# Attention with chosen key chunks and a gated FFN on one core: the first pairs' k and q loaded three tokens side by side and turned head by head, the guard value as a step of its own, and a new order of the steps

## The chip, the cores and the metric

The kernel runs on one core of a Trainium2 chip. The core has five engines with instruction streams of their own: TensorE (PE in the profile, with PEld for its weight loads), VectorE (DVE), ScalarE (ACT), GpSimd (POOL) and SyncE (SP). SP, ACT and POOL also issue DMA transfers, which run on 16 DMA engines. The metric is device time of one execution in microseconds (us). Three runs of the kernel before took 319.53, 315.69 and 314.50 us, median 315.69.

## The reference

There are 4 batches of 8 heads, 768 tokens and head size 64. Keys are cut into 24 chunks of 32. For every query an upper bound of its score with each chunk is worked out from the smallest and largest key of the chunk; the six chunks with the highest bounds are kept, and attention runs over those alone, causally. The result, 3072 tokens by 512, goes through a normalisation and a gated FFN of width 1536.

```python
k_min, k_max = np.min(k_chunks, axis=3), np.max(k_chunks, axis=3)
ub = np.sum(np.maximum(q * k_min, q * k_max), axis=-1)      # per query and chunk
ub = np.where(causal, ub, -1e9)
top_chunks = np.argsort(ub, axis=-1)[..., -6:]
scores = scale * (q @ k.T);  mask = sel & (pos[:, None] >= pos[None, :])
attn = softmax(np.where(mask, scores, -1e9));  x = attn @ v
xn = x / sqrt(mean(x * x) + 1e-6) * rms_g
out = (silu(xn @ w_gate) * (xn @ w_val)) @ w_out
```

## The kernel before, in words

The work is cut into 16 pairs of heads, four pairs to a batch, and the FFN into eight halves of a batch (384 tokens each). Every piece of work is a "step" with a name, an engine or a choice of engines, the steps it depends on and the buffers that it opens and uses. The order of the steps, the engine of each and the slot of each new buffer stand in one long text, PROGRAM (lines 28 to 149): "P153:6" is step 153 on TensorE with its buffer in slot 6, and A, D, G and S are ACT, DVE, POOL and SP. `Order.run` follows the text word by word. Each engine runs its own steps in that order. So an engine never overtakes in its own queue, and a step that waits holds up everything behind it on the same engine.

For each pair, `prep` does the following.

- **Load** (L497): k and q of both heads come in as [128 partitions, 6 tiles, 2 heads, 64 values] in fp32. Partition p of tile t holds token 128 t + p, so one contiguous piece is the 64 values of a token, 256 bytes. Pair 0 is loaded in two halves, one head from SP's queue and the other from ACT's; the other pairs have one DMA a head from SP. The buffers of kind "nat" have 7 slots.
- **Turn** (L517): three tiles go into one PSUM bank by three fp32 transposes of 128 by 128 (both heads at once), which gives the head's values on the partitions and tokens along the row. There are two such banks in a tensor. They are evicted to SBUF (helper `evict`, L289 on ACT and L293 on DVE or POOL) as "kt" and "qt".
- **Bounds**: smallest and largest key of each chunk (L546, L548, DVE), their difference (`dif`, L599), the positive part of q ("relu", L633 on ACT or L635 on DVE), then small fp32 matmuls "ub" (L723; L781 for two pairs at once from pair 6 on). The ub matmuls use parts of the array: 64 rows (a head) by 32 columns, six or eight of them side by side. The bounds are copied out, turned back ("up", L747 or L803), and the causal mask is added (L762, L810).
- **Choice**: MAX8 finds the eight highest bounds (L650). The step "sel" then does two things on DVE: it compares each bound with the sixth highest (L665 or L674), and it writes one more column, the guard value max(highest - 480, 0) (L668 or L679).
- **Placing the choice**: for pairs 0 to 2 TensorE turns the choice ("selT", L694) and DVE copies it beside the query values ("selC"). From pair 3 on, q is laid out by a cast ("qN"), the choice is written beside it, and a DMA transpose (L557) turns both together; that buffer, "qn", has two slots. The keys carry matching constant rows (`e_all`; SP copies them at L385 and L386 into the sets of buffers that pairs use).

`scores` then makes score groups of up to 512 columns (L868, with the triangular mask of batch 0 added by a matmul at L874), exponentials on ACT (L885) and the products with v (L904). The v loads are DMAs that POOL issues (L473), and so are the six weight loads (L437 for gate and value, L442 for out). `norm` and `ffn` work batch by batch: gate steps L1037, value steps L1058, out steps L1078.

Fillers (L338) are matmuls on a tile of zeros. There are 88 such steps to choose from, and PROGRAM may leave them out; this one uses 34. All other work of TensorE is needed.

Of the kernel before, what the change touches and what calls it, by code (L numbers as in the profile page):

```python
# [198 lines left out]
def kernel(  # L199
# [25 lines left out]
    W = S // 2  # L225
    G = 3
    DUO = 6
    KSIDE, QM = 16, 3
    HW = NT * P + D
    NPAIRS = B * NP  # L230

# [51 lines left out]
    def pe(n):  # L283
        return 0.003 + n / 2400.0
# [56 lines left out]
    for i in range(BUSY):  # L341
        bank = Buf("ps")
        add("busy", "PE", pe(4 * P), 1000.0 + i, busy(bank, 4 * P), [c_zero], opens=[bank])
# [806 lines left out]
```

## Time and profile before

| | |
|---|---|
| runs shown | 314.50, 315.69, 319.53 us |
| the profiled execution | 314.75 us, of which the instructions span 313.0 |
| TensorE busy | 303.2 us, 97% |
| DVE, ACT, POOL busy | 231.5, 185.5, 103.9 us |
| granted TensorE clock | 0.997 of full |
| read from HBM, written | 28.57 MB, 6.29 MB |

A group line of the page gives the source line, engine and operation, what is written and read with its shape, then how often, the busy time in us, the mean in ns, and the idle time of the engine before it with what ended it. A timeline line gives start and length in us, and in brackets idle time with its releaser. In the table by stretches the columns are TensorE, its weight loads, DVE, ACT and POOL with counts, then the granted clock, the mean number of busy DMA queues for an engine, and GB/s. Lengths of matmuls overlap: the next one starts before the one before has ended, so their number and the chain say more than the sum of lengths.

### The profile page before, as it was taken

To read this page: it belongs to the slowest core of one execution; us is meant where nothing else is said; L and a number is where in the kernel's file an instruction comes from. 1 tells how busy PE (TensorE), PEld (TensorE's weight loads), DVE (VectorE), ACT (ScalarE), POOL (GpSimd) and SP (SyncE) were. 2 spreads that over 40 slices of the span, in tenths; PEclk is the share of its full clock that TensorE was granted. 3 is DMA by queue.
4 is the path that set the end of the run, shared out by engine and by line. 5 is a ranking of instruction groups with operands and counts; after the bars stand their busy time and mean duration, and the time that the engine had idled before them with its cause. 6 is when DMAs were issued, how large, how long until landed. Compare 5 with 4: busy or idle time off the path is not lost.

```text
span 313.0 us, 7431 instructions
## 1 busy us (share of the span) xinstructions
PE 303.2 (97%) x2772; PEld 191.7 (61%) x2790; DVE 231.5 (74%) x654; ACT 185.5 (59%) x415; POOL 103.9 (33%) x162
## 2 busy tenths in 40 slices
PE   7998999999999999999999999999999999999994
PEld 3676776576576855667687546656666545555541
DVE  4998989969985789856978879989544564577551
ACT  1688998783298773697794643366697403442001
POOL 8686453371354843252377100033233110000000
PEclk9999999999999999999999999999999999999998
DMA  9999999999699996797684060361240034100014
GB/s 173 220 190 126 96 191 206 201 165 168 129 185 198 220 114 146 175 191 138 138 68 28 17 140 13 52 77 36 58 79 36 2 78 155 69 3 0 2 67 169
DMA packets 113301, 35.35 MB, mean 113 GB/s; under 512 B 106225, under 2 KB 110065, under 8 KB 113265
## 3 DMA queue, kind: packets, MB, share of 16 engines
q1 hardware_dynamic: 83152, 26.62, 41.1%
q0 software_dynamic: 28512, 7.87, 24.9%
q10 hardware_dynamic: 1600, 0.39, 0.6%
q8 instruction: 22, 0.36, 0.5%
q14 instruction: 15, 0.11, 0.1%
HBM read 28.57 MB, written 6.29 MB: 111 GB/s over the span
## 4 chain that ended last, share of the span: by engine, by line
PE 87%; DMA 5%; DVE 4%; POOL 1%; issue 1%; SPq 1%; ACT 1%; POOLq 0%
PE po L1078 20%; PE vp L1058 19%; PE gp L1037 19%; PE sc L868 9%; PE av L904 5%; DMA wv<-in_moe_w_val_dram 4%; PE pk L517 3%; PE busy L338 3%; PE pq L517 3%; PE ub L781 2%; PE ub L723 2%; PE up L803 1%; DMA qs<-qn 1%; DVE m L650 1%; DVE qs L293 1%
## 5 line engine op out<-in xcount | busy, mean ns | idle before, releaser
L885 ACT ACTIVATE pt<-sc 128x512 bf16<-128x512 f32 (+2 forms) x192 | 92.9, 561 | 17.5 <-PE sc L868 15.4
L1044 ACT ACTIVATE sg<-gp 128x384 bf16<-128x384 f32 x96 | 45.5, 496 | 55.1 <-PE gp L1037 42.2
L1050 DVE SCALAR_TENSOR_TENSOR tg<-sg,gp 128x384 bf16<-128x384 bf16 x96 | 51.8, 550 | 32.0 <-ACT sg L1044 30.6
L1058 PE MATMUL vp<-xT,wv 128*128 128x384 bf16 x384 | 74.0, 326 | 0.3 <-DMA wv<-in_moe_w_val_dram 0.2
L1037 PE MATMUL gp<-xT,wg 128*128 128x384 bf16 x384 | 73.2, 326 | 0.7 <-ACT xT L289 0.4
L1078 PE MATMUL po<-wo,hh 128*128 128x512 bf16 x272 | 66.9, 379 | 0.9 <-issue 0.2
L1066 DVE TENSOR_TENSOR hh<-vp,tg 128x384 bf16<-128x384 f32 x96 | 51.6, 552 | 12.6 <-PE vp L1058 11.7
L868 PE MATMUL sc<-qs,ke 128*128 128x128 bf16 (+5 forms) x420 | 57.1, 251 | 0.3 <-DMA qs<-qn 0.2
L1058 PEld LDWEIGHTS <-wv 128*128 128x128 bf16 x384 | 35.9, 98 | 25.0 <-issue 1.2
L1037 PEld LDWEIGHTS <-wg 128*128 128x128 bf16 x384 | 36.2, 98 | 23.9 <-issue 1.5
L1078 PEld LDWEIGHTS <-hh 128*128 128x128 bf16 x288 | 27.3, 98 | 29.1 <-issue 1.5
L904 PEld LDWEIGHTS <-pt 128*128 128x128 bf16 x672 | 35.1, 98 | 10.5 <-ACT pt L885 0.6
L904 PE MATMUL av<-vx,pt 128*128 128x65 bf16 x672 | 41.4, 193 | 0.1
L891 POOL TENSOR_SCALAR_AFFINE_SELECT pt<-pt 128x512 bf16<-128x512 bf16 (+1 forms) x48 | 24.4, 521 | 47.4 <-ACT pt L885 43.6
L868 PEld LDWEIGHTS <-ke 128*128 128x128 bf16 (+1 forms) x420 | 30.6, 97 | 9.6 <-issue 1.6
L293 POOL CAST ke<-kt 64x768 bf16<-64x768 f32 x32 | 26.6, 835 | 16.6 <-ACT kt L289 6.0
L293 POOL CAST qn<-qnat 128x768 bf16<-128x768 f32 x13 | 10.7, 822 | 40.5 <-DMA qs<-qn 40.5
L291 ACT ACTIVATE osb<-po 128x512 f32<-128x512 f32 x12 | 7.1, 599 | 24.7 <-PE po L1078 24.7
L981 DVE SCALAR_TENSOR_TENSOR xs<-xb,ri,gains 128x512 bf16<-128x512 bf16 x24 | 17.5, 751 | 2.1 <-POOL ri L973 1.7
L925 DVE TENSOR_TENSOR xb<-av,rden 128x384 bf16<-128x384 f32 (+1 forms) x34 | 18.2, 534 | 1.2
L473 POOL DMA_DIRECT2D vx<-in_v_dram x16 | 16.9, 1055 | 0.1
L650 DVE MAX8 m<-ubm 128x8 f32<-128x8 f32 (+4 forms) x192 | 16.7, 160 | 0.2
(83 smaller groups left out, 297.7 us busy)
## 6 DMA issues: line engine op xcount, KB each, us to landing
out_dram<-osb SPq DMA_DIRECT2D x24, 256.0 KB, 2.3
knat<-in_k_dram SPq DMA_DIRECT2D x30, 192.0 KB, 4.3
qnat<-in_q_dram SPq DMA_DIRECT2D x30, 192.0 KB, 4.6
vx<-in_v_dram POOLq DMA_DIRECT2D x16, 192.0 KB, 5.5
wg<-in_moe_w_gate_dram POOLq DMA_DIRECT2D x2, 768.0 KB, 11.6
wv<-in_moe_w_val_dram POOLq DMA_DIRECT2D x2, 768.0 KB, 10.0
wo<-in_moe_w_out_dram POOLq DMA_DIRECT2D x2, 768.0 KB, 10.1
qs<-qn SPq DMA_TRANSPOSE x26, 2.8
```

The costliest lines, as they stand in the source:

```text
L293: engine[e].tensor_copy(out_, in_)
L650: nc.vector.max(out=m8.tile[:, y[0], y[1], :], in_=ubm.tile[:, y[0], y[1], 0:max(8, 4 * (i0 + x) + 4)])
L868: nc.tensor.matmul(t[:, x:x + m, :].rearrange("p a b -> p (a b)"), ke[kk, kb * P:(kb + 1) * P], qs[kk, q0 * P:(q0 + m) * P], start=not tri ...
L885: nc.scalar.activation(out=t[:, 0:nn, :], in_=sc.tile[:, 0:nn, :], func=ACT.Exp, scale=SCALE)
L891: nc.gpsimd.affine_select(out=pt.tile[:, 0:nd, :], in_=pt.tile[:, 0:nd, :], compare_op=ALU.is_ge, fill=0.0, base=0, pattern=[[0, nd], [1, ...
L904: nc.tensor.matmul(av.tile[:, qi - i0, :], pt.tile[:, x, :], VX[c.v.slot][:, hl * NT + kb, :], start=(begin and m == 0), stop=(left[0] == ...
L1037: nc.tensor.matmul(t[:], wg[:, g, hs], XT[b].tile[:, g, cols], start=(g == 0), stop=(g == NP - 1))
L1044: nc.scalar.activation(out=t[:], in_=gp.tile[:], func=ACT.Tanh, scale=0.5)
L1050: nc.vector.scalar_tensor_tensor(out=t[:], in0=sg.tile[:], scalar=1.0, in1=gp.tile[:], op0=ALU.add, op1=ALU.mult)
L1058: nc.tensor.matmul(t[:], wv[:, g, hs], XT[b].tile[:, g, cols], start=(g == 0), stop=(g == NP - 1))
L1066: nc.vector.tensor_tensor(out=t[:], in0=vp.tile[:], in1=tg.tile[:], op=ALU.mult)
L1078: nc.tensor.matmul(po.tile[:], hhs[ht].tile[:, th * P:(th + 1) * P], wo[:, ht, :], start=(ht == 0), stop=(ht == NHT - 1))
```

## The change

There are four parts.

1. k of pairs 0 to 3 and q of pairs 0 to 2 are loaded so that partition p of a group of 384 tokens holds the tokens 3p, 3p+1 and 3p+2 one after the other: one contiguous piece has 768 bytes.
2. Those tensors are turned by plain fp32 matmuls against the identity in place of transposes: for each of three columns of tokens and each head, 64 stationary columns on 128 moving ones, head 0 into the columns 0 to 63 of the array and head 1 into 64 to 127. That is six matmuls a bank in place of three. The eviction puts the columns back in the order of tokens, writing every third column.
3. The guard value leaves "sel" and becomes a step "grd", which ACT, POOL or DVE may do. ACT needs a constant column `cap` of -480 for it.
4. POOL may do "relu", and PROGRAM is a new one.

Also new is a way to load v through SP and a cast; its list of pairs, VDIRECT, is empty, so it isn't used.

The new order uses 6 fillers, all at the beginning. Its first loads are q and k of pair 0 by halves in turn, q and k of pair 1, k of pair 2, q of 3, k of 6, k of 3; the constant key rows come behind these, where before they stood behind the loads of pair 1 and k of 3. TensorE turns k of pair 0, one bank of q of pair 1, q of pair 0, k of pair 1 and a bank of k of pair 2 ahead of the first "ub"; by the first score it has turned ten banks of k and seven of q, where the order before has eight and four. Of the guards 5 are on ACT, 9 on POOL and 2 on DVE; 5 relus are on POOL, 8 on ACT (12 before) and 3 on DVE (4 before). POOL issues both gate loads, then a q cast, then the first value load; before it was gate, value, gate, behind that cast. The FFN begins with 7 gate steps instead of 4.

```diff
+    K3, Q3 = 4, 3
+    VDIRECT = ()
...
+    cap = const.tile([P, 1], FP32, name="cap")
+    c_cap = add("cap", "DVE", 0.07, -98, lambda e: nc.vector.memset(cap[:], -GUARD))
...
+            three = p < (K3 if w == "k" else Q3)
...
+                if three:
+                    if nat[w].tile is None:
+                        tile_of(nat[w], [P, NT // 3, 2, 3 * D], FP32, w + "nat")
+                    for hl in range(2):
+                        eng = nc.scalar if p == 0 and hl else nc.sync
+                        eng.dma_start(out=nat[w].tile[:, r0 // 3:(r0 + rn) // 3, hl, :],
+                                      in_=src[b, h0 + hl, r0 * P:(r0 + rn) * P].rearrange(
+                                          "(g p s) d -> p g (s d)", p=P, s=3))
+                    return
...
+                    if three:
+                        for j in range(3):
+                            for h in range(2):
+                                nc.tensor.matmul(
+                                    t[h * D:(h + 1) * D, j * P:(j + 1) * P],
+                                    nat[w].tile[:, j0 // 3, h, j * D:(j + 1) * D], ident_f[:],
+                                    start=True, stop=True, tile_position=(0, h * D))
+                        return
...
+                    if three:
+                        evict(e, big[w].tile[:, j0 * P:(j0 + 3) * P].rearrange("p (x s) -> p s x", s=3),
+                              bank.tile[:].rearrange("p (s x) -> p s x", s=3))
+                        return
...
-                nc.vector.tensor_scalar(
-                    out=s12[:, :, NCH:NCH + 1], in0=m12[:, :, 0:1], scalar1=-GUARD,
-                    scalar2=0.0, op0=ALU.add, op1=ALU.max)
...
+            def guard(e):
...
+                o, m = s12[:, :, NCH:NCH + 1], m12[:, :, 0:1]
+                if e == "ACT":
+                    nc.scalar.activation(out=o, in_=m, func=ACT.Relu, bias=cap[:, 0:1])
+                else:
+                    engine[e].tensor_scalar(out=o, in0=m, scalar1=-GUARD, scalar2=0.0,
+                                            op0=ALU.add, op1=ALU.max)
...
-            sT = add("selT", "PE", nb * 0.057, rank(at, b, "selT"), sel_turn, [pk, c_idb], opens=[st], uses=[sq])
+            sT = add("selT", "PE", nb * 0.057, rank(at, b, "selT"), sel_turn, [pk, gd, c_idb], opens=[st], uses=[sq])
```

More of the change, by code (lines that the diff above doesn't have):

```diff
@@ L470, in load_v, with get @@
         b, h0 = c.b, c.h0
+        if c.p in VDIRECT:
+            vn = Buf("nat")
+            def get(e):
+                t = tile_of(vn, [P, 2 * NT, D], FP32, "vnat")
+                nc.sync.dma_start(out=t[:], in_=v[b, h0:h0 + 2].rearrange("h (t p) d -> p (h t) d", p=P))
+            x = add("vget", "SP", 1.0, rank(lr, b, "vload"), get, opens=[vn], load=S * 550)
+            c.vload = add("vC", "", {"POOL": pool(2 * NT * D), "DVE": 0.5, "ACT": act(2 * NT * D)},
+                          rank(lr, b, "vload"), lambda e: evict(e, VX[c.v.slot][:, :, 0:D], vn.tile[:]),
+                          [x] + c_vx, opens=[c.v], uses=[vn], port=True)
+            return
         def go(e):
@@ L503, in prep @@
                           lambda e, load=load, r0=r0: load(e, r0=r0, rn=3), opens=[nat[w]],
-                          load=3 * P * 550) for r0 in range(0, nb, 3)]
+                          load=3 * P * (380 if three else 550)) for r0 in range(0, nb, 3)]
             else:
                 ld = [add(w + "load", "SP", 1.4, rank(lr, b, w + "load"), load, opens=[nat[w]],
-                          load=n * 550)] * 2
+                          load=n * (380 if three else 550))] * 2
             ready[w] = ld
@@ L519, in turn @@
                             nat[w].tile[:, j0 + j].rearrange("p h d -> p (h d)"), ident_f[:])
-                tr = add(w + "T", "PE", 0.33, rank(at, b, w + "T", j0, "step"), turn, [ld[j0 // 3], c_id],
+                tr = add(w + "T", "PE", 0.83 if three else 0.33, rank(at, b, w + "T", j0, "step"), turn, [ld[j0 // 3], c_id],
                          opens=[bank], uses=[nat[w]])
@@ L634, in relu @@
             else:
-                nc.vector.tensor_scalar(out=t[:, 0:n], in0=big["q"].tile[:, 0:n], scalar1=0.0,
+                engine[e].tensor_scalar(out=t[:, 0:n], in0=big["q"].tile[:, 0:n], scalar1=0.0,
                                         scalar2=None, op0=ALU.max)
-        rl = add("relu", "", {"DVE": 0.07 + n * 0.00056, "ACT": act(n)}, rank(at, b, "relu"), relu, done["q"], opens=[rel],
+        rl = add("relu", "", {"DVE": 0.07 + n * 0.00056, "ACT": act(n), "POOL": pool(n)}, rank(at, b, "relu"), relu, done["q"], opens=[rel],
                  uses=[big["q"]], port=True)
@@ L686, in choose @@
             if side_q:
-                c.sel = turned(QN, qn, QS, "qX", [pk, qs_n])
+                c.sel = turned(QN, qn, QS, "qX", [pk, gd, qs_n])
                 return c.sel
```

21 lines of the change are left out of this document (14 added, 7 removed), and 245 rows, old and new, of the table PROGRAM.

## The prediction

> **What bounds the kernel now.** I read the page first: its engine totals, its slices and the chain of work that ended last.
>
> ```profile
> PE 303.2 (97%) x2772; PEld 191.7 (61%) x2790; DVE 231.5 (74%) x654; ACT 185.5 (59%) x415; POOL 103.9 (33%) x162
> PE   7998999999999999999999999999999999999994
> DMA  9999999999699996797684060361240034100014
> PE 87%; DMA 5%; DVE 4%; POOL 1%; issue 1%; SPq 1%; ACT 1%; POOLq 0%
> ```
>
> TensorE is busy 97% of the span and carries 87% of the chain. So a gain must take time off TensorE's own instruction stream, or out of its idle time. The second view, busy time in 10 us stretches, says where idle time is.
>
> ```profile
> 0.00:10.00 10.00, 7.80 (x32) 3.92 (x33) 4.94 (x14) 3.42 (x6) 6.84 (x18) 1.00 1.02 184
> 10.00:20.00 10.00, 9.95 (x115) 6.46 (x114) 9.43 (x38) 6.13 (x14) 8.66 (x16) 1.00 1.25 209
> 20.00:30.00 10.00, 8.83 (x121) 6.15 (x119) 9.05 (x28) 8.99 (x21) 6.22 (x9) 1.00 1.26 162
> 30.00:40.00 10.00, 9.73 (x143) 7.66 (x142) 9.52 (x30) 9.46 (x23) 4.74 (x6) 1.00 0.99 84
> 40.00:50.00 10.00, 9.90 (x172) 8.47 (x173) 8.83 (x22) 9.46 (x23) 5.17 (x8) 1.00 1.11 202
> 50.00:60.00 10.00, 9.56 (x64) 5.44 (x62) 9.82 (x34) 7.33 (x18) 2.60 (x3) 1.00 1.12 198
> 60.00:70.00 10.00, 9.59 (x113) 6.51 (x111) 7.45 (x15) 9.11 (x20) 8.06 (x12) 1.00 1.27 180
> ```
>
> The first number after the length is TensorE. It idles 2.20 us before its first instruction, then 0.05, 1.17, 0.27, 0.10, 0.44 and 0.41 us to 70 us. From 10 to 60 us DVE is 88 to 98% busy and from 20 to 50 us ACT is at 90 to 95%, so in this stage three engines are nearly full at once. But "busy" hides one thing: fillers (L338), matmuls on zeros that keep TensorE running while nothing useful is ready. The third view, the chain in order of time, has them and the prices that I need below.
>
> ```profile
> 2.20 5.24 PE busy L338 x12
> 7.76 0.66 PE pq L517 x6
> 8.74 1.29 PE busy L338 x6
> 11.12 1.01 PE ub L723 x24
> 73.17 1.45 PE ub L781 x32
> ```
>
> Twelve fillers take 0.437 us each at the start, and six of the same form 0.215 each from 8.74 us: TensorE runs at half speed for its first 5 us or so, though the granted clock is 1.00 throughout. The kernel issues 34 fillers (32 are in the records): 12 x 0.437 + 22 x 0.215 = 9.97 us that compute nothing. Idle time and fillers before 70 us, 14.6 us in all, are what a better beginning can win. After that TensorE is full.
>
> **The change, part by part.** Counts come from the order of the two kernels' instructions.
>
> *Fillers.* 34 become 6, all at the start: 6 x 0.437 = 2.62 us. Removed: 7.35 us. This is a gain only so far as useful work stands where they stood. If their cover is gone, the wait shows as idle time of the same length; the turning below is what fills it.
>
> *Turning.* Four k tensors and three q tensors (14 banks of 384 columns) go from three fp32 transposes a bank, 0.33 us by the row at 7.76, to six fp32 matmuls of 64 stationary columns on 128 moving ones, the two heads in the two halves of the array. No row shows this form. The nearest is ub: six small fp32 matmuls side by side, every one recorded twice, so that 24 records are four rounds of 256 columns (1.01 us) and 32 are four rounds of 384 (1.45 us). The difference, 0.44 us for 512 columns, gives 0.11 us a round of 128 columns and 0.13 us once for starting. A bank is three column blocks of two rounds: 6 x 0.11 = 0.66 us, if both heads run in the same round. The 14 banks stand in five runs: 14 x 0.66 + 5 x 0.13 = 9.9 us, against 14 x 0.33 = 4.6: 5.3 us more. Lower bound 4.6 (starts hidden); it can't be a gain, since twice the matmuls stream the same columns. Upper bound: heads one after the other, 14 x 1.32 + 0.65 - 4.6 = 14.5. I take 5.3, since ub's six run side by side.
>
> *Half speed.* The six fillers end at 2.20 + 2.62 = 4.8 us, and the first two banks follow while TensorE is still slow (in the trace to about 7.4 us): 2 x 0.66 = 1.3 us more. Bounds 0 and, if it stays slow to the first score, some 11 us (below).
>
> *Loads.* Rows of 768 bytes in place of 256, a third of the packets.
>
> ```profile
> DMA packets 3413, 0.87 MB, mean 218 GB/s; under 512 B 3412, under 2 KB 3412, under 8 KB 3412
> DMA packets 402, 0.73 MB, mean 121 GB/s; under 512 B 48, under 2 KB 48, under 8 KB 402
> GB/s 410 396 219 0 0 0 0 0 0 0 0 0 0 0 0 0 341 396 382 341 410 396 410 341 396 82 0 0 0 0 0 0 0 0 0 0 0 0 14 300
> ```
>
> The first row is 14 to 18 us, all but one 256-byte packets, at 218 GB/s; the other two are the output stores at 303 to 309 us, about 2 KB each, at some 396 GB/s when they move. Per engine (of 16) that is 18.8 and 82.8 ns a packet; a line through both gives 37 ns for 768 bytes, 330 GB/s. A tensor of 393 KB takes 1.2 us instead of 1.8, seven of them 4.3 us less of a queue that is full to 27 us. On the path I count nothing: no wait of TensorE in the first 20 us is put down to a load; behind the fillers it follows DVE and ACT. What it buys is that later tensors are there to be turned where fillers stood. Bounds: 0 and 0.5 us at the first tensor.
>
> *Evictions.* They write every third column.
>
> ```profile
> L293 DVE COPY qt<-pq 128x384 f32<-128x384 f32 x9 | 4.9, 551 | 1.8 <-PE pq L517 1.8
> L289 ACT ACTIVATE kt<-pk 128x384 f32<-128x384 f32 x23 | 11.5, 513 | 5.2 <-PE pk L517 5.1
> L546 DVE TENSOR_REDUCE kmx<-kt 128x24 f32<-128x768 f32 x15 | 14.2, 944 | 0.0
> ```
>
> Before, 0.55 us on DVE and 0.51 on ACT. I add 0; bounds 0 and as much again for each of the 14, of which three stand on the first pair's path. The third row is for the first score, below.
>
> *The guard value.* It leaves the DVE step "sel" and becomes a step of its own, 5 on ACT, 9 on POOL, 2 on DVE.
>
> ```profile
> 15.12 0.87 DVE L674 SCALAR_TENSOR_TENSOR selq<-m,ubm 128x288 bf16<-128x288 f32 x1
> 15.73 0.94 POOL L293 CAST qs<-qt 64x768 bf16<-64x768 f32 x1
> 15.91 0.81 DVE L679 TENSOR_SCALAR selq<-m 128x12 bf16<-128x12 f32 x1
> 16.78 0.34 PEld L694 LDWEIGHTS <-selq 128*128 128x128 bf16 x6 [0.20 <-DVE selq L679]
> 18.34 0.94 PE L868 MATMUL sc<-qs,ke 89*128 89x512 bf16 x8
> 18.62 1.22 POOL L473 DMA_DIRECT2D vx<-in_v_dram  x1
> 21.80 0.51 PE L694 MATMUL st<-ident_b,selq 128*128 128x128 bf16 x6 [0.38 <-DVE selq L679]
> 24.74 0.65 PE L723 MATMUL ub<-qt,ku 64*32 64x256 f32 x12 [0.79 <-DVE qs L293]
> L679 DVE TENSOR_SCALAR selq<-m 128x12 bf16<-128x12 f32 x3 | 2.4, 812 | 0.0
> L668 DVE TENSOR_SCALAR qn<-m 128x12 bf16<-128x12 f32 x13 | 2.9, 225 | 0.0
> ```
>
> Twelve values a lane take 0.81 us in the first three pairs and 0.23 in the others: the long ones start inside a POOL cast and end with it (16.72 against 16.67). On DVE 2.4 + 2.9 us go, less two at 0.2. On the path it is 0.81 us less a parallel 0.25 for pair 0, which TensorE waits for at 16.78 and 21.80. On POOL a guard stands behind what is queued there: for pair 1, the dif of pair 3 and two v loads of about 1.2 us each (18.62), and the turn of its selection waits for it; but its DVE max is due no earlier, so I add 0 (bound 1 us). One memset on DVE comes in, some 0.1 us at the start, behind longer ones.
>
> *Other moves.* Five relus go to POOL (about 0.9 us there, as its cast above), off ACT and DVE. On SP the four copies of the constant key rows go behind four more loads; pair 1's scores need them only after pair 0's, so 0. POOL issues the two gate loads before, and the first value load after, the third q cast, which must wait for a DMA transpose to free its buffer (4.81 us in the first row).
>
> ```profile
> 40.25 0.85 POOL L293 CAST qn<-qnat 128x768 bf16<-128x768 f32 x1 [4.81 <-DMA qs<-qn]
> 41.87 0.70 POOL wg L437
> 42.57 11.57 DMA wv<-in_moe_w_val_dram
> 51.19 2.76 PE L1037 MATMUL gp<-xT,wg 128*128 128x384 bf16 x16
> 54.19 1.47 PE L1058 MATMUL vp<-xT,wv 128*128 128x384 bf16 x8 [0.24 <-DMA wv<-in_moe_w_val_dram]
> 60.85 0.81 PE L1037 MATMUL gp<-xT,wg 128*128 128x384 bf16 x4 [0.41 <-ACT xT L289]
> ```
>
> Before, the FFN had 4 gate steps to run before values; now 7, 3 x 0.69 (a quarter of 2.76) = 2 us more cover.
>
> *Idle time.* From 10 to 70 us it is 2.44 us. The guard's wait (0.38), half of that behind the selection copies (0.79 at 24.74), and the waits at 54.19 (0.24) should go: 0.9. Late next is the first score. Before it starts at 18.34 us (row above). After, ub of pair 0 starts at about 11.9 instead of 11.12 (half-speed turning, six more banks ahead of it), its eviction stands on DVE behind two reductions of pair 1 (2 x 0.94 us, less what they overlap: 1.6), and the guard gives 0.7 back: about 20.0. That is no loss by itself, because three banks of pairs to come are turned by then.
>
> *The sum*, on TensorE's stream: -7.35 (fillers) + 5.3 (turning) + 1.3 (half speed) - 0.9 (idle) = -1.65 us. The profiled execution took 314.75 us with a span of 313.0, so 313.1. It lies 0.9 below the median of the three runs, 315.69, between them and the lowest. I say 313.0.
>
> **A rule weighed.** TensorE's weight loads decide the upper bound.
>
> ```profile
> L517 PEld LDWEIGHTS pq<-ident_f,qnat 128*128 128x128 f32 x96 | 10.7, 141 | 1.8 <-issue 0.8 <-ACT pt L885 0.2
> ```
>
> A load of 128 fp32 columns takes 141 ns, yet six transposes take 0.66 us, 110 ns each: the loads run under matmuls that use all rows of the array, as both heads do here. The Trainium skill, "TensorE: Matmul & The Clock Gate", Part 3, The mechanism, says that weight loads overlap running matmuls only when their row groups differ; by that rule no load of the new turning would hide. Its row here speaks against it, for whole-array loads; no row shows loads into half the columns.
>
> **The rivals.**
> 1. *The heads don't run side by side* (slower). Turning costs 14.5 instead of 5.3 and its slow start twice: 313.1 + 9.2 + 1.3 = 323.6. For it: no row has two matmuls that share all rows and differ in columns; by the rule above, exposed loads lead to about the same. Against it: ub's groups share halves of the rows and run in one round by their price. It passes 2% over the median when a bank costs over 1.27 us. Chance 0.12.
> 2. *TensorE stays at half speed* (slower). 28 fillers go from the stage before the first score. What stands there afterwards is about 13 us at full speed; 11 of it again would give 324, and the bound of 2% is passed when half speed lasts 9 us of work longer. Against it: the stream has no gap over 1 us in my reckoning. The same page, Part 4, says that transposes don't count as activity for the clock; by that rule matmuls in their place would help here. Chance 0.08.
> 3. *The waits go as well* (faster). Turning at its lower bound 4.6, no half-speed loss, and all 2.44 us of idle time gone with 0.6 of the start: 314.75 - 7.35 + 4.6 - 3.0 = 309.0. For it: the waits at 16.78, 21.80 and 24.74 end in DVE, which loses some 5 us of guards. Against it: DVE and ACT are still nearly full. Chance 0.20.
> 4. *The early stage hangs on DVE, ACT and POOL* (no change). Idle time takes the place of the fillers: the first score 1.7 us late is not made up, or the value weights, now behind a cast that waits for a DMA, land 1 to 2 us late: 315 to 316. Chance 0.12.
>
> **How the numbers follow.** Forecast 313.0, chance 0.48; its own range, by 4.6 to 7 us of turning and 0 to 2.4 of idle time, is 311 to 316. The range that should hold 8 in 10 goes down to rival 3 with half a us beyond, 308.5, and up past rival 4 to 319.0, leaving out rivals 1 and 2 (0.20). A difference of 2%, 6.3 us, is about what a measurement of this kernel can tell from no change. Faster than 309.4: most of rival 3 and a tail of the forecast, 0.20. Slower than 322.0: rivals 1 and 2 and a tail, 0.22. Within: 0.58.
>
> **What would show it.** Turning: a bank of twelve records in 0.66 to 0.8 us, heads in pairs; rival 1 shows 1.3. Fillers: 6 records, at 0.437. Half speed: the first two banks at 1.3 us; rival 2 if ub takes 2 us at 12 us. Loads: some 330 GB/s before 8 us. Guard: no DVE row of 0.81, selection's turn no longer waiting for it. First score near 20 us, first gate step near 50.5, first value step without a wait. The forecast is wrong if idle time to 70 us exceeds 5 us, or if TensorE loses time after 70 us, where I count nothing.

## The result and the profile after

| | before | after |
|---|---|---|
| median of 11 runs each, us | 315.68 (313.72 to 319.53) | 318.05 (317.51 to 319.78) |
| ratio of the times, 95% interval | | 1.0102, 1.0077 to 1.0126 |
| the profiled execution, its span, us | 314.75, 313.0 | 317.64, 315.8 |

The change makes the kernel 1.0% slower, 3.2 us by the ratio, where 0.8% faster was forecast. That is inside the 2% that I called no change and inside the range, but on the other side. Ratios compare executions in the usual state; two of the eleven of one run below (e5) were in a slower one and are left out.

First the page of the changed kernel: totals, the slices of TensorE, and the chain by engine.

```profile
PE 301.7 (96%) x2871; PEld 192.8 (61%) x2888; DVE 229.6 (73%) x646; ACT 186.0 (59%) x411; POOL 117.8 (37%) x175
PE   6899999899989999999989989999999999999994
PE 79%; DMA 12%; DVE 3%; SPq 2%; issue 1%; ACT 0%; ACTq 0%; POOL 0%
```

TensorE's share of the chain fell from 87 to 79%, and the share of DMA rose from 5 to 12%. The slices have 8s in the middle, where the kernel before had 9s throughout. Two rows for each kernel say how much that is: before, then after, then a run that comes below (e9, value loads in other places). The first number behind the length is TensorE's busy time.

```profile
0.00:70.00 70.00, 65.36 (x746) 1.00 1.15 174
70.00:300.00 230.00, 228.91 (x1989) 1.00 0.55 93
```

```profile
0.00:70.00 70.00, 64.49 (x852) 1.00 1.14 189
70.00:300.00 230.00, 225.48 (x1977) 1.00 0.56 88
```

```profile
70.00:300.00 230.00, 229.05 (x2010) 1.00 0.54 89
```

Up to 70 us the idle time is 4.64 us before and 5.51 after. From 70 to 300 us it is 1.09 before and 4.52 after: 3.43 us more in a stage in which I counted nothing. The stretches of 10 us of the changed kernel, as shown of before, and those later ones in which idle time appears:

```profile
0.00:10.00 10.00, 7.25 (x78) 4.71 (x80) 6.32 (x16) 2.84 (x4) 6.85 (x20) 1.00 0.81 224
10.00:20.00 10.00, 8.70 (x141) 6.83 (x141) 7.75 (x27) 7.43 (x14) 7.05 (x11) 1.00 1.00 224
...
80.00:90.00 10.00, 9.22 (x89) 5.88 (x88) 7.04 (x18) 8.14 (x17) 5.49 (x9) 1.00 1.42 146
150.00:160.00 10.00, 8.77 (x88) 6.42 (x86) 9.17 (x18) 7.71 (x19) 6.11 (x9) 1.00 0.84 100
180.00:190.00 10.00, 8.61 (x54) 5.12 (x53) 6.96 (x15) 2.94 (x7) 4.73 (x5) 1.00 1.39 119
```

The beginning of the changed kernel, from the timeline of TensorE:

```profile
1.24 2.74 PE L339 MATMUL busy<-zeros 128*128 128x512 bf16 x6 [1.24 <-DVE zeros L334]
4.12 0.88 PE L545 MATMUL pk<-ident_f,knat 128*64 128x128 f32 x12
6.28 0.88 PE L545 MATMUL pk<-ident_f,knat 128*64 128x128 f32 x12 [1.29 <-DMA knat<-in_k_dram]
14.52 0.52 PE L551 MATMUL pk<-ident_f,knat 128*128 128x128 f32 x3 [1.15 <-DMA knat<-in_k_dram]
16.25 2.19 PE L545 MATMUL pk<-ident_f,knat 128*64 128x128 f32 x36
21.34 0.83 PE L917 MATMUL sc<-qs,ke 89*128 89x512 bf16 x4
56.59 0.82 PE L1107 MATMUL vp<-xT,wv 128*128 128x384 bf16 x4 [0.98 <-DMA wv<-in_moe_w_val_dram]
```

Three banks in a row take 2.19 us, the last one to its own end, so some 0.7 us a bank. TensorE now waits for loads (1.29 and 1.15 us), and the first value step waits for its weights. The late waits, two answers of the timeline and one row each:

```profile
87.29 0.93 PE L917 MATMUL sc<-qs,ke 89*128 89x128 bf16 x8 [0.36 <-DMA qs<-qn]
158.75 0.39 PE L917 MATMUL sc<-qs,ke 128*128 128x384 bf16 x2 [1.23 <-DMA qs<-qn]
187.56 0.81 PE L1086 MATMUL gp<-xT,wg 128*128 128x384 bf16 x4 [1.40 <-DVE xs L1030]
```

The last one reads "xs" on VectorE, but that step is only what ended last in the profile: this gate step needs three blocks of xT, which come by transposing DMAs. The third of them was issued at 181.5 us and landed 6.0 us later, at 187.5; the gate step starts at 187.56. So all three waits hang on transposes that SP issues. The view of the DMAs gives their time from issue to landing (last column) and what else is in flight, first before, then after, each for 78 to 94, 146 to 160 and 176 to 190 us.

```profile
qs<-qn SPq DMA_TRANSPOSE x6, 2.8
qs<-qn SPq DMA_TRANSPOSE x4, 2.7
xT<-xs SPq DMA_TRANSPOSE x6, 2.6
```

```profile
qs<-qn SPq DMA_TRANSPOSE x5, 5.7
qs<-qn SPq DMA_TRANSPOSE x4, 4.0
vx<-in_v_dram POOLq DMA_DIRECT2D x2, 192.0 KB, 6.1
xT<-xs SPq DMA_TRANSPOSE x6, 4.6
```

These are medians; they are 1.3 to 2.9 us longer than before. The timelines of POOL and SP of the changed kernel say what has moved next to them:

```profile
80.38 1.11 POOL L489 DMA_DIRECT2D vx<-in_v_dram  x1
85.12 1.03 POOL L489 DMA_DIRECT2D vx<-in_v_dram  x1
151.89 1.11 POOL L489 DMA_DIRECT2D vx<-in_v_dram  x1
180.46 2.10 POOL L489 DMA_DIRECT2D vx<-in_v_dram  x2
```

```profile
148.95 5.88 SPq L595 DMA_TRANSPOSE qs<-qn  x4
178.88 9.89 SPq L1041 DMA_TRANSPOSE xT<-xs  x6
```

Each late wait has value loads issued by POOL among the transposes. The kernel before issues its loads at 155.27 and 156.90 us, behind the four transposes of that place, and none between 167 and 204 us; from 78 to 89 us it has one, at 84.12, where the changed kernel has two.

### The profile page after: what moved, and what is told of

Read it like the earlier page. It is cut to its first block, busy times and chain, and to the rows that moved or that the text cites. A ratio compares the mean times of both kernels' runs of the same rounds, so it can differ in the third digit from the quotient of the medians.

```text
span 315.8 us, 7625 instructions
## 1 busy us (share of the span) xinstructions
PE 301.7 (96%) x2871; PEld 192.8 (61%) x2888; DVE 229.6 (73%) x646; ACT 186.0 (59%) x411; POOL 117.8 (37%) x175
## 4 chain that ended last, share of the span: by engine, by line
PE 79%; DMA 12%; DVE 3%; SPq 2%; issue 1%; ACT 0%; ACTq 0%; POOL 0%
PE po L1127 19%; PE vp L1107 18%; PE gp L1086 17%; PE sc L917 9%; PE av L953 5%; DMA wv<-in_moe_w_val_dram 4%; DMA qs<-qn 4%; DMA qnat<-in_q_dram 3%; PE ub L830 2%; PE pk L551 2%; PE pq L551 2%; DMA knat<-in_k_dram 2%; SPq L523 2%; PE ub L772 1%; PE up L852 1%
## 5 line engine op out<-in xcount | busy, mean ns | idle before, releaser
L1086 PE MATMUL gp<-xT,wg 128*128 128x384 bf16 x384 | 74.2, 326 | 1.5 <-DVE xs L1030 1.4
L953 PEld LDWEIGHTS <-pt 128*128 128x128 bf16 x672 | 32.8, 98 | 10.0 <-issue 0.6
L953 PE MATMUL av<-vx,pt 128*128 128x65 bf16 x672 | 38.3, 193 | 0.3 <-DMA vx<-in_v_dram 0.3
L917 PEld LDWEIGHTS <-ke 89*128 89x128 bf16 (+1 forms) x420 | 30.7, 97 | 12.8 <-DMA qs<-qn 2.5
L294 POOL CAST ke<-kt 64x768 bf16<-64x768 f32 x31 | 25.5, 827 | 25.8 <-PE sc L917 12.7
L292 ACT ACTIVATE osb<-po 128x512 f32<-128x512 f32 x14 | 8.4, 601 | 23.1 <-PE po L1127 22.3
L296 DVE TENSOR_SCALAR osb<-po 128x512 f32<-128x512 f32 x10 | 6.9, 688 | 15.9 <-PE po L1127 15.9
L1022 POOL TENSOR_TENSOR ri<-ms,mhalf 128x3 f32<-128x3 f32 x8 | 7.4, 928 | 29.3 <-DVE ms L1014 29.3
```

The lines of the kernel that those rows point to most:

```text
L294: engine[e].tensor_copy(out_, in_)
L917: nc.tensor.matmul(t[:, x:x + m, :].rearrange("p a b -> p (a b)"), ke[kk, kb * P:(kb + 1) * P], qs[kk, q0 * P:(q0 + m) * P], start=not tri ...
L953: nc.tensor.matmul(av.tile[:, qi - i0, :], pt.tile[:, x, :], VX[c.v.slot][:, hl * NT + kb, :], start=(begin and m == 0), stop=(left[0] == ...
L1086: nc.tensor.matmul(t[:], wg[:, g, hs], XT[b].tile[:, g, cols], start=(g == 0), stop=(g == NP - 1))
```

## The experiments

I call the runs by short names, h1 to h4 and e5 to e19 (there is no e15). Ratios are to the kernel before on the same chip. Step numbers are the changed kernel's; "the order before" is before's PROGRAM in these numbers.

### Which part of the order costs: two joins

```diff
 PROGRAM of h1: the changed kernel's words up to "D1304:7" (about 75 us), then
-S497 P1298:3 D1351:3 ...      the changed kernel's rest
+P431 P444 P452 ...            the order before, without what is done; guard on D
 PROGRAM of h2: the order before up to its first transpose of pair 5, then the
 changed kernel's rest; K3, Q3 = 0, 0
```

> The changed kernel's steps, in its order, up to the issue of the first transposing DMA of pair 5 (about 75 us; three-token loads, side-by-side turning, 6 fillers, guard on the engines that the change chose), and from there the order and engines of the kernel before, with the guard a step of its own on VectorE right ahead of or behind the selection. Theory T (the new beginning gains about 0.9 us, and the loss is three waits of TensorE in the new order behind 80 us, 1.3 + 1.4 + 1.6 us): about 0.9 us under the kernel before, 314.8 us beside 315.7, ratio 0.997. Rival R1 (the loss belongs to the new loads and turning, whose cost shows late): as the changed kernel, 318 us, ratio 1.008. Rival R2 (any join of two orders costs as much as the waits): over 317 us.

Measured: 316.12 us, ratio 1.0026 (1.0007 to 1.0045). The new start with the old rest is 2.4 us faster than the changed kernel, so most of the loss lies behind 75 us, as theory T said. But the start gains nothing either: T's 0.9 us is missed by 1.7.

> The opposite join: the kernel before's steps, in its order and with its loads (two tokens of 64 values for each row, heads turned one after another, 34 fillers), up to the first transposing DMA of pair 5, and from there the changed kernel's order and engines. Theory T: the three late waits stay and the beginning's 0.9 us is not gained: 3.3 to 4.3 us over the kernel before, about 319.5 us, ratio 1.012. Rival R1 (loads and turning cost it): as the kernel before, 315.7 us, ratio 1.000.

Measured: 325.04 us, ratio 1.0296 (1.0262 to 1.0330). (The expectation describes the kernel before wrongly: it loads one token of 64 values in a piece and turns both heads at once.) The direction is T's, the size is not. The join put more waits in, and one of them cost twice. TensorE's timeline, and its clock in stretches of 2 us (the figure behind POOL's):

```profile
188.23 2.11 PE L1109 MATMUL vp<-xT,wv 128*128 128x384 bf16 x12
192.72 1.04 PE L1088 MATMUL gp<-xT,wg 128*128 128x384 bf16 x4 [2.05 <-DVE xs L1032]
194.20 3.29 PE L1088 MATMUL gp<-xT,wg 128*128 128x384 bf16 x12
```

```profile
194.00:196.00 2.00, 2.00 (x8) 1.01 (x7) 1.56 (x5) 0.78 (x2) 0.00 (x0) 0.50 0.00 0
```

The wait that took 1.40 us in the changed kernel takes 2.05 here, and from about half a us behind it the granted clock is 0.50: twelve matmuls take 3.29 us in place of 2.11. So h2 shows that the late wait comes with the new rest; as a price of it, it is of no use.

### Loads and turning apart from the order

```diff
 h3, the changed kernel:          h4, the order before, guard on D:
-    K3, Q3 = 4, 3               -    K3, Q3 = 0, 0
+    K3, Q3 = 0, 0               +    K3, Q3 = 4, 3
```

> The changed kernel with its whole order, but the first pairs loaded and turned as in the kernel before. TensorE turns 14 banks at 0.33 us in place of 0.66, 4.6 us less work before 35 us, while the loads come in smaller pieces and there are still only 6 fillers. Theory T (late waits cost the time, and the beginning was short of data, not of TensorE): the waits for the first loads grow by as much as the turning falls, and the time stays at 317 to 319 us. Rival R1 (the turning is what costs): 4.6 us under the changed kernel, 313.4 us.

Measured: 319.35 us, ratio 1.0128 (1.0099 to 1.0157). In the new order the old loads and turning are no better, 0.8 us worse with overlapping intervals. T holds, with a time a little over its range, and R1 falls: taking 4.6 us of turning away bought nothing there. In the trace TensorE waits for loads instead: up to 70 us it is idle for 10.39 us, where the changed kernel is for 5.51. The granted clock, too, is 0.50 from 8 to 10 and from 18 to 20 us in this execution (320.12 us); the three with a clock of 1.00 throughout took 318.4 to 318.7.

> The kernel before's whole order, its 34 fillers included, with the new loads and side-by-side turning, and the guard a step of its own on VectorE. The turning is 4.6 us more TensorE work in the first 35 us and the fillers stay. By T: 2 to 4.6 us over the kernel before (the waits for loads in its beginning, 2 to 3 us, give some of it back), 317.7 to 320.3 us. If the turning were hidden behind the loads: 315.7 us, ratio 1.000.

Measured: 320.44 us, ratio 1.0160 (1.0130 to 1.0190). Against the same order with old loads (e14, below, 0.9996) that is 1.64% or 5.2 us, some 4 to 6.4 with both intervals and a little over what T gave. Loads and evictions changed with the turning, so this is the price of the three together; no run has the turning alone.

### The value loads

```diff
 POOL's words in e5 (the other engines' words are untouched; G498 is v of pair 5,
 G576 of 7, G840 of 10, G981 of 12, G999 of 13, G1122 of 14, G1140 of 15)
-G451 G571 ... G574 G498 G522 G572 G526 G576 G712
+G451 G498 G576 G571 ... G574 G522 G572 G526 G712
-G977 G840 G836 ... G949 G997        +G977 G836 ... G949 G840 G997
-G945 G1140 G903                     +G945 G981 G903
-G1118 G1122 G1600                   +G1118 G999 G1600
-G1135 G999 G981 G1139 G1138 G1120   +G1135 G1139 G1138 G1122 G1140 G1120
 e9: as e5, but G1122 G1140 behind G1086
```

> The changed kernel, and only the places of seven value loads in POOL's order are others: pairs 5 and 7 some 10 us earlier (before the transposing DMAs of pairs 5 to 7), pair 10 some 4 us later (behind those of pairs 10 and 11), pairs 12 and 13 in the places of 15 and 14, and 14 and 15 behind the transposing DMAs of pair 13, so that none is issued among the transposes for 186 us. TensorE, VectorE, ScalarE and SyncE have the changed kernel's order. Theory V (value loads sent by POOL while transposing DMAs are in flight make these land in 4.0 to 5.7 us in place of 2.6 to 2.8, and TensorE waits for them at 81 to 92, 157 and 186 us): the waits of 1.7 + 1.4 + 1.6 us fall to about 1.5 in all, 315 us, ratio to the kernel before 0.998. Rival P (TensorE is sent to these products too early, whatever the loads do): 317 to 318 us, ratio 1.005 to 1.008.

Measured: 318.88 us (316.25 to 322.06), ratio 1.0090 (1.0053 to 1.0127): by the number, rival P. The profiled execution, at 322.06 us, is the slowest of the eleven: TensorE waited 2.46 us at 14 to 16 us and then had a clock of 0.50 to about 22 us. So I took only one thing from it: the waits at 157 and 186 us were gone, and a new one stood where I had put the loads of pairs 14 and 15, among the transposes of pairs 12 and 13.

```profile
206.89 0.38 PE L917 MATMUL sc<-qs,ke 128*128 128x128 bf16 x4 [2.05 <-DMA qs<-qn]
```

> As the first run with values away, but the loads of pairs 14 and 15 are issued behind the first masks of pair 13 (about 207 us), no longer between the transposing DMAs of pairs 12 and 13 and their landing, where the first run had a new wait of 2.2 us. Theory V: the waits at 157, 186 and 204 us are all gone, 80 to 92 us keeps under 1 us; with a beginning like the changed kernel's in its profile 314 to 315 us, ratio to the kernel before 0.995 to 0.999. Rival P (the order waits anyway, at another place): 316.5 us or more, ratio over 1.003.

Measured: 316.15 us, ratio 1.0020 (0.9995 to 1.0044), against 1.0102 of the changed kernel. Seven words on POOL give back 0.8%, 2.6 us (with both intervals, some 1.5 to 3.7). The idle time from 70 to 300 us is 0.95 us (the row at the top), and the same transposes land about as before, here at 146 to 160 and 176 to 192 us:

```profile
qs<-qn SPq DMA_TRANSPOSE x4, 2.7
xT<-xs SPq DMA_TRANSPOSE x6, 2.4
```

The third transpose of xT, which landed in 6.0 us in the changed kernel, lands in 2.4. The time lies between the two forecasts (V 0.995 to 0.999, P over 1.003), and the trace decides for V: nothing else was changed, TensorE's order, which rival P blamed, is the same, and its waits are gone. What each of the seven loads is worth by itself was not tried. What is left over the kernel before belongs to the beginning (e16, below).

> The changed kernel with the value loads where they were, and ten of TensorE's steps moved behind work that is ready: four score steps of pairs 6 and 7, three of pair 10 and the first three gate steps of the third block, each behind 1 to 2 us of other products. By V and by P alike the waits at 87, 91, 157 and 186 us are covered: 2.5 to 4 us under the changed kernel, 314 to 315.5 us, ratio 0.995 to 1.000. Rival R3 (ScalarE, VectorE and the banks get the scores later, and TensorE waits for them as long a little later): 317 to 318 us.

```diff
 PROGRAM, TensorE's words: P598 P623 behind P523; P665 P661 behind P1320; P640 P651
 behind P1359; P915 P901 behind P972; P888 behind P956; P1607 P1627 P1617 behind P1539
```

(Three words of ACT and DVE moved with these.) Measured: 320.14 us, ratio 1.0147 (1.0095 to 1.0199). R3 holds, and worse. TensorE waits elsewhere: 0.68 and 0.37 us at 164 to 166 us for ScalarE, which gets the scores late, and for a value load:

```profile
91.17 0.41 PE L953 MATMUL av<-vx,pt 128*128 128x65 bf16 x8 [1.06 <-DMA vx<-in_v_dram]
```

> The value loads as in the run with values away, and three waits of the new beginning covered: pair 0's first query bank is turned between its two key banks, pair 6's first key bank behind pair 1's last query bank, and the loads of the value and output weights are issued ahead of POOL's cast for pair 5 and of its 2.1-us rectifier for pair 5. If the waits seen in the changed kernel's beginning (1.3, 1.15 and 1.07 us) are TensorE's own time: 2 to 3 us under the run with values away, about 312.5 us, ratio 0.990. If the beginning hangs on the loads' total and the waits only move: as the run with values away, ratio 0.998.

```diff
 e5, and: P84 behind P90; P544 behind P107; G77 ahead of G485;
 G79 G80 (second loads of value and out weights) ahead of G486 and G427
```

Measured: 333.75 us, ratio 1.0580 (1.0525 to 1.0635), a miss by 21 us. Four things were changed at once, so the time has no single cause, but the two longest waits fit theory V, here with loads of weights. Two loads of 768 KB now leave POOL at 57.5 and 58.3 us, up to 2 us behind the issue of the transposes of pair 4. Its timeline, and the landing times from 52 to 78 us:

```profile
67.77 2.32 PE L917 MATMUL sc<-qs,ke 128*128 128x512 bf16 x16 [4.23 <-DMA qs<-qn]
76.00 0.87 PE L551 MATMUL pk<-ident_f,knat 128*128 128x128 f32 x3 [4.63 <-DMA knat<-in_k_dram]
```

```profile
knat<-in_k_dram SPq DMA_DIRECT2D x2, 192.0 KB, 15.7
qs<-qn SPq DMA_TRANSPOSE x2, 8.2
```

In the changed kernel the same two took 3.9 and 4.5 us (50 to 62 us); there the two large loads leave at 58.8 and 59.6 us, about when the transposes, issued from 52.7 us on, have landed. Behind these waits the granted clock of e7 falls as well, to 0.67 on average from 70 to 80 us.

> All three edits together: values away, scores later, waits of the beginning covered. If each wait is TensorE's own: 311.5 to 313 us, ratio 0.987 to 0.992, faster than both kernels. If the moved score steps only pass the wait on (R3): as the run with values away and the early edits.

The edits of e5, e6 and e7 together. Measured: 333.98 us, ratio 1.0599 (1.0555 to 1.0643), the same as e7.

> The run with pair 6 later, and the first loads of the gate and value weights issued ahead of POOL's 2.1-us rectifier of pair 4 (at 38 in place of 40.3 to 43.7 us), so that the first gate and value steps at 52 to 57 us do not wait for them (0.3 to 1.0 and 1.1 to 1.2 us). No transposing DMA is issued between 34 and 52 us. If that wait is theirs alone: 1 to 2 us under the run with pair 6 later, about 311.5 us, ratio 0.987. If the loads of queries 5 to 7, which the weights then meet, pass it on: no difference.

```diff
 e10 (below), and POOL's words
-G415 G76 G78 G485 G77
+G76 G78 G77 G415 G485
```

Measured: 329.25 us, ratio 1.0447 (1.0401 to 1.0493); neither forecast comes near. The weights left POOL at 37.5 to 39.0 us in place of 40.3 to 43.7, in the middle of the issue of q of pairs 7, 6 and 5 (35.3 to 40.9 us), and one of these became the wait:

```profile
55.66 0.87 PE L551 MATMUL pq<-ident_f,qnat 128*128 128x128 f32 x3 [11.56 <-DMA qnat<-in_q_dram]
```

In this wait, from 48 us on, the granted clock is 0.50, and it stays so to about 61.5 us; that is part of the time lost.

### The beginning

> The second run with values away, and the turning of pair 6's first key bank behind pair 1's last query bank and the first transposed sums of pair 0 (in the changed kernel TensorE stands 1.15 to 2.6 us before it at 13 to 16 us, and in the run in which it stood 2.6 us its clock fell to half until about 28 us). If that stall is TensorE's own and sets off the clock: 1 to 2 us under the second run with values away, and less spread: 312.5 to 313.5 us. If the beginning is bound by the loads: no difference.

```diff
 e9, and TensorE's words
-P104 P338 P544 P160 P107 P333
+P104 P338 P160 P107 P544 P333
```

Measured: 315.73 us, ratio 1.0011 (0.9981 to 1.0041), no difference to e9 that can be told. (In the run meant above, e5, the wait was 2.46 us and the clock was at half until about 22 us, not 28.) The trace says little, since the stall before pair 6 is not in e9's trace either: there the banks ahead of it run late. In e10's trace 0.72 us for a copy on VectorE and 0.43 us for a load stand behind that place. By the forecast this speaks for a beginning that is bound by its loads; it isn't shown.

> The kernel before's order with its loads, turning and fillers; only the guard is a step of its own, on the engine that the changed kernel gives it (POOL nine times, ScalarE five, VectorE two). By all theories 315 to 316.5 us, ratio 0.998 to 1.003: VectorE's 16 times 0.4 us lie beside TensorE's work. If the guard's place in the chain of selection costs TensorE: 317 us or more.

```diff
 the order before, K3, Q3 = 0, 0, and the guards' words
+A111 G179 G247 G354 G423 G494 G588 A594 G735 A729 A876 D870 A1011 G1017 D1158 G1152
```

Measured: 314.38 us, ratio 0.9962 (0.9937 to 0.9988). The guard alone gains 1.2 us, more than all theories had.

> The kernel before's order, the guard a step of its own, but on VectorE right behind or ahead of the selection, as before. If the gain of the guard alone (1.2 us) comes from taking 0.4 us sixteen times off VectorE: as the kernel before, 315.3 to 316 us, ratio 0.999 to 1.001. If it comes from the split itself, or is chance: 314.4 us, ratio 0.996.

All sixteen of these words with D. Measured: 315.17 us, ratio 0.9996 (0.9973 to 1.0019), as before. So the gain goes with the engine and not with the split, as far as two intervals that overlap a little can tell. The traces say where it comes from: the two waits of TensorE behind VectorE that the prediction shows at 21.80 and 24.74 us are still in e14 (0.38 us at 21.51 and 0.79 at 24.45) and are gone in e11. From 14 to 30 us TensorE is busy for 14.83 us before and in e14, and for 15.88 in e11.

> The run with the guard alone (old order, old loads, old turning), with only its first 6 of 34 fillers. The forecast's sum took 7.35 us off for them. If fillers are TensorE's own time: 5 to 7 us under the run with the guard alone, 308 us, ratio 0.977. Theory F (TensorE waits for the first loads where it ran fillers): no gain, 314 to 316 us, ratio 0.995 to 1.002, and idle time in their place before 24 us. If the idle time lets the clock fall: over 316 us.

```diff
 e11 without 28 of the 34 "busy" words
```

Measured: 313.08 us, ratio 0.9927 (0.9899 to 0.9955), the fastest kernel of the study, faster than both. Against e11 the 28 fillers give 0.35%, 1.1 us; the intervals overlap, and with both it is nothing to 2.3 us. Theory F holds. Where they stood, TensorE waits or is slow:

```profile
6.04 0.87 PE L552 MATMUL pk<-ident_f,knat 128*128 128x128 f32 x3 [1.08 <-DMA knat<-in_k_dram]
6.71 1.49 PE L552 MATMUL pq<-ident_f,qnat 128*128 128x128 f32 x6
7.99 2.33 PE L552 MATMUL pk<-ident_f,knat 128*128 128x128 f32 x9
10.24 1.07 PE L773 MATMUL ub<-qt,ku 64*32 64x256 f32 x12
```

Eighteen transposes take 4.2 us from 6.04 to 10.24, at 0.11 us each they would take 2.0. Up to 70 us TensorE is busy for 63.35 us, in e11 65.87: 2.5 us more idle time.

> The run with the fillers out, and the first 6 out as well. If the clock has to be woken by work: the first five banks run at half speed, 0.14 us more each for three turns, and the time is 0.7 to 1.5 us over the run with the fillers out, 314 to 314.6 us, ratio 0.995 to 0.998. If the clock is up by the time of the first bank anyway, or TensorE waits for loads there: no difference, 313.1 us, ratio 0.993.

e13 without the other six. Measured: 313.46 us, ratio 0.9942 (0.9918 to 0.9967): no difference to e13. The first bank stands at 5.91 us and runs at the same slow pace as in e13, so there six fillers with 1.08 us of idle time behind them woke nothing.

> The changed kernel's beginning (to the issue of pair 5's first transposing DMA), then the order of before with the guard on the changed kernel's engines: it differs from the run with the guard alone in the beginning only. If the new beginning gains what the forecast said (1.65 us): 312.7 us, ratio 0.991. If its fillers were no time of TensorE's and the turning is: 315.5 to 316.5 us, ratio 1.000 to 1.003.

h1 with the guards' letters of e11. Measured: 316.53 us, ratio 1.0036 (1.0013 to 1.0059). Against e11, from which only the start differs, that is 0.74%: the new beginning costs 2.3 us. From h1 it differs only in the engine of the last eight guards, and the two times can't be told apart (1.0026 and 1.0036): this fits a gain in the first pairs, as the waits of e14 have it.

> The same, with pair 6's first key bank turned behind pair 1's last query bank. If the stall before it (1.15 to 2.6 us) is TensorE's own: 0.5 to 1.5 us under the run with the new start and the guard, about 315 us. If the next bank is as late: no difference.

e16 with e10's edit. Measured: 316.30 us, ratio 1.0019 (0.9993 to 1.0044). No difference that can be told.

> The run with the fillers out (old order, 6 fillers, guard on the changed kernel's engines), with the changed kernel's loads and side-by-side turning for the first pairs. If the turning is TensorE's own time even where it waits for loads: 5 us over the run with the fillers out, 318 us, ratio 1.009. Theory F (TensorE has about 2 us of waits for loads there before 16 us, and the larger pieces land sooner): 2 to 3.5 us over it, 315 to 316.5 us, ratio 0.999 to 1.003. If the earlier data are worth more than the turning: under 313 us.

e13 with K3, Q3 = 4, 3. Measured: 316.72 us, ratio 1.0032 (1.0003 to 1.0061): 1.05%, 3.3 us over e13, at the upper end of theory F. The twelve executions lie far apart (314.30 to 318.47 us), and in the profiled one, at 318.45, part of the loss isn't turning:

```profile
52.65 4.44 PE L1087 MATMUL gp<-xT,wg 128*128 128x384 bf16 x16 [0.69 <-ACT xT L291]
```

The same sixteen matmuls take 2.76 us in e13. The granted clock is 0.50 from 53 to 56 us, behind four waits of 0.61, 0.27, 0.27 and 0.69 us. How much of the 3.3 us this is in the other executions isn't known. By the median it is as slow as e16: the old order with 6 fillers and the new loads does as well as the newly searched beginning.

## Why the prediction was wrong

From the ratios the 3.2 us of loss fall into three: the guard on other engines -1.2 us (e11), the new beginning +2.3 (e16 against e11), the new order behind it +2.1 (after against e16). Each is uncertain by about 1 us. Step by step:

- **After 70 us, "where I count nothing"**: this step failed. I had named two signs of a wrong forecast, lost time behind 70 us and over 5 us of idle time up to there, and both came. I looked at what the order does around the diff and not at which DMAs it puts beside which, 80 us and more behind it. The value loads among the transposes cost 2.6 us (after against e9). The Trainium skill, "DMA: Bandwidth & Descriptors", section "Queues, rings and completion order", says that each DMA engine takes the queues that have work in turn, a packet from each; the traces agree in direction, 2.7 us for a transpose without and 4.0 with a value load in flight, though they do not show the turns themselves.
- **Fillers, -7.35 us**: the step that failed in the beginning. Removing 28 fillers is worth 1.1 us (e13 against e11), nothing to 2.3 with the intervals. I wrote that the gain holds only so far as useful work stands there, and then took all of it because the turning would fill it. In e13 2.5 us came back as idle time, and 2.6 as slow pace (2.2 for the transposes, 0.4 for ub); the sum counts the same time as waiting and as gain. That no wait of the first 20 us was put down to a load held only with the fillers there: without them a bank waits 1.08 us for its load in e13. Fillers and turning together were forecast at -2.05 us and measured at +2.2. (Not all 28 stood ahead of the first score, as rival 2 has it: in the records of before 28 of all 32 do, so 22 went from there.)
- **Turning, +5.3 us**: right where fillers stay, 5.2 us in the old order (h4 against e14), though loads and evictions are in that number. A bank takes 0.71 to 0.73 us with its share of the starts (from 16.25 to 18.37 us three in the changed kernel, 1.46 us for two in h4), as the sum's 9.9 us for 14 banks has it, and heads run in pairs; rival 1 is out. With fewer fillers 3.3 us are left (e18 against e13); that the rest stands in waits is the likely reason, not a shown one.
- **Half speed, +1.3 us**: not there in the profiled execution of the changed kernel. The zeros are ready at 1.24 us, not 2.20, so the fillers start 1 us earlier, and the first two banks take 0.88 us each (the rows at 4.12 and 6.28). That is luck of this execution: in the other traces with the same first steps the first bank takes 1.4 to 1.6 us, and the two together 0.8 us (e16), 1.4 (h1) and 1.5 (e9) more than here. So the term was about right for most of the traces. The rows of e9 are below. Rival 2, half speed up to the first score, is out: ub takes 0.65 us there, as before.
- **Loads**: they move 286 GB/s from 4 to 10 us, 330 was the estimate. But nothing on the path was too little: TensorE waits 1.29 and 1.15 us for them, which no filler covers any more.
- **Guard**: the 0.81 us rows are gone, as forecast. ACT and POOL take 0.34 us each, 0.43 in two cases on POOL. I gave the guard one of the waits behind VectorE and half of the other; both are gone in e11, and by itself the guard is worth 1.2 us.
- **Relus on POOL, about 0.9 us**: they take 2.14, and one of them stands ahead of the weight loads. No run puts a price on that; moving the loads ahead of it did harm (e12).
- **Evictions, 0**: 0.12 to 0.19 us longer each, inside the bound.
- **Idle time, -0.9 us**: it grew, 5.51 us to 70 us in place of 4.64. Of rival 4, the value weights came 0.98 us late and the first score at 21.34 us in place of 20.0; the first gate step came at 50.63, as forecast.

```profile
L724 ACT ACTIVATE qn<-m,cap 128x12 bf16<-128x12 f32 x4 | 1.4, 344 | 2.5 <-DVE m L688 2.5
L726 POOL TENSOR_SCALAR qn<-m 128x12 bf16<-128x12 f32 x7 | 2.4, 340 | 19.8 <-DVE m L688 19.7
L673 POOL TENSOR_SCALAR rt<-qt 128x768 f32<-128x768 f32 x5 | 10.7, 2141 | 4.3 <-DVE ku L637 2.0 <-ACT qt L290 1.2 <-DVE qt L294 1.1
```

These are the groups for the guard and the relu, with the mean of one in ns behind the busy time. The first two banks of the same beginning in e9:

```profile
3.91 1.55 PE L545 MATMUL pk<-ident_f,knat 128*64 128x128 f32 x12
6.02 1.72 PE L545 MATMUL pk<-ident_f,knat 128*64 128x128 f32 x12 [0.56 <-DMA knat<-in_k_dram]
```

By the measured prices the beginning comes to -1.2 (guard) - 1.1 (fillers) + 3.3 (turning and loads, with part of the turning inside waits) = +1.0 us against the kernel before. For e18 this is so by the way the prices were taken; e16 is a measurement of its own, with the new order of these steps, and has +1.1. The forecast had -1.65 there.

What stays open: which of the new beginning's waits and slow stretches makes its price, since the same first steps gave waits of other lengths in every trace (for pair 0's second key bank 1.29 us in the changed kernel, 0.56 in e9 and 0.27 in e10, and e10's and e17's edit changed nothing that can be told), and whether the transposes are slowed by the number of packets or by the bytes beside them; that was not tried.

## What to carry to other kernels

The length of a filler is not what its removal gains: before taking it off a sum, ask what TensorE would wait for without it, and take off only what has useful work ready at that moment. When an order is searched anew, compare for every DMA that somebody waits for what else is in flight beside it, over the whole span and not only around the edit: here seven loads in other places cost about as much as the whole new beginning. And when transfers share the DMA engines, issuing a large one earlier is not free: three of them 3 to 5 us earlier cost 13.8 us (e12 against e10). And one trace of a beginning isn't its price: ask for the spread before calling a term absent.

## What the runs showed of the hardware that was not expected

- Transposing DMAs land later beside value and weight loads. With no value load issued among them their medians are 2.4 to 3.2 us (e9, and before but for one place), with one or two of 192 KB 4.0 to 5.7 (after), and with two loads of 768 KB issued behind them 8.2 (e7). In the kernel before, the one value load among transposes leaves at 84.12 us: the two transposes issued at 83.0 and 84.3 us take 3.6 and 5.1 us, the four others from 78 to 94 us 2.5 to 2.8.
- A single idle time of 2.05 us was followed by a clock of 0.50 for about 3 us (h2), while 1.40 us at the same place was not (after). The Trainium skill, "TensorE: Matmul & The Clock Gate", Part 1, gives about 3.4 us of idle time for that; this run shows it at less. These runs give no limit to keep to: four waits of 0.61, 0.27, 0.27 and 0.69 us were followed by 0.50 in e18, and 0.50, 0.27, 0.27 and 0.69 us ahead of the same step in e13 were not.
- The granted clock does not tell the slow start: in e13 and e19 it reads 1.00 to 12 us, while transposes take 0.21 to 0.25 us each to 10 us and, behind that, one ub takes 1.07 us and the next 0.64 (e13).
- Writing every third column costs at the eviction: 0.67 us on VectorE (at 6.25 us of the changed kernel) and 0.70 on ScalarE (at 8.42), in place of 0.55 and 0.51.
